# Four output groups in another order, and seven gate multiplications on GpSimd instead of VectorE

## The chip, the cores and the metric

The kernel runs on one core of a Trainium2 chip. The metric is the device time of one execution in microseconds (us), lower being better. The core's engines work side by side, each through its own queue in order: TensorE (PE in the profile, with PEld for its weight loads), VectorE (DVE), ScalarE (ACT), GpSimd (POOL) and SyncE (SP), which here only issues DMAs. A queue's own waiting and issuing is written with a q (SPq).

## What is computed

The input x has 2048 positions of 512 numbers in bfloat16. It is normalised, goes through two blocks side by side, and their sum is added to x:

```
xn = layernorm(x)
A: qkv = xn @ wqkv;  32 heads of 16; each position attends to 8 positions, 0, 2, ... 14 back
   o = softmax(q k / 4) v;           A = o @ wo
B: z = gelu(xn @ w_in)               (1376 wide, two halves of 688)
   z1 = first half;  z2 = layernorm(second half)
   g = w_sp @ z2 + b_sp              (w_sp is 2048 x 2048, mixing positions)
   B = (z1 * g) @ w_out              (688 to 512)
out = x + A + B
```

## The kernel before

Positions are worked in 16 tiles of 128. What matters here is the last third: the mixing of positions, the second half of the attention, and the output.

**Order.** Every step is a named operation, written down by `op_(name, needs, f)`. Five hand-written lists, `pe`, `act`, `dve`, `pool` and `sp`, hold the order of each engine's queue (lines 594 to 641). An engine works through its list in order; if one step waits, those behind it in the list wait too. The letters used below are the names in these lists.

**Mixing and gates.** `M{j}` (line 479) are the 32 matmuls of tile j of w_sp @ z2, into one of three PSUM tiles (`mm`). `G{j}` (ScalarE, line 495) adds the bias and copies the result to one of three gate buffers (`gs`), so `G{j}` needs `g{j-3}` done. `g{j}` (line 497) multiplies the gate with z1, 128 x 688 in bfloat16, in place in `z1u`; before the change all 16 are VectorE's. `U{j}` (line 484) is a DMA transpose, issued by SP, of the product into `uT`, with the 688 features on partitions: five full blocks of 128 and a rest of 48. `V{th}{g}` (line 490) are small DMAs that spread the rest rows over four partition groups (`rest`): those of the first half of the positions (th = 0) are issued by GpSimd, those of the second half by SP.

**Attention.** The positions are two halves, th = 0 and 1. VectorE multiplies the attention weights with the values and sums them in twelve steps `a{th}.0` to `a{th}.11` (lines 430, 434 and 443). The last, line 443, writes `op`, which lies in the place of `xnT`; the profile shows it by that name. All operands are in SBUF. Between these steps stand the `g{j}` in VectorE's list.

**Output.** The 16 output tiles are four groups of four; group n = 2 th + s. Each tile of a group has its own PSUM bank; groups 0 and 2 share four banks, groups 1 and 3 the other four. A tile is the sum of three parts:
- the full gated part (`gated_full`, line 533): five matmuls over 128 x 512 from `uT` and `w_out`;
- the gated rest (line 540): two small matmuls per tile with 32 and 16 rows;
- the attention part (line 544): 16 small matmuls per tile with 32 rows from `op` and `wo`. The small matmuls of a group's four tiles stand at four row positions of the array.

In the old order PE's list ends with gf0 gf1 ao0 ao1 gf2 ao2 ao3 gf3: full parts of groups 0 and 1; rest and attention parts of 0 and of 1; full part of 2; rest and attention of 2 and of 3; the full parts of group 3, whose last tile is done in three column pieces (`gfl0` to `gfl2`, line 567) in banks that have come free. `ao{n}` holds rest and attention parts together. ScalarE copies the finished groups 0 and 1 out (`E{i}`, line 578), and VectorE adds x to the copies (`F{i}`, line 579); for groups 2 and 3 VectorE adds x straight from PSUM (line 584). VectorE's additions stand behind all attention steps in its list. SP stores each tile (line 585).

Of the kernel before, what the change touches and what calls it, by code (L numbers as in the profile page):

```python
# [10 lines left out]
ALU = mybir.AluOpType  # L11
# [5 lines left out]
NT = S // P  # L17
# [9 lines left out]
FH = 688  # L27
F = 2 * FH
# [14 lines left out]
def kernel(  # L43
# [13 lines left out]
    V = nc.vector  # L57
    A = nc.scalar
    G = nc.gpsimd
# [23 lines left out]
    b16 = sb.tile([NT, P], BF16, name="b16")  # L83
# [21 lines left out]
    gs = [qk_r[0][:, (MF + 1) * HS + n * FH:(MF + 1) * HS + (n + 1) * FH] for n in range(3)]  # L105
# [8 lines left out]
    z1u = z1_r[:].rearrange("p (i f) -> p i f", i=NT)  # L114
# [38 lines left out]
    def op_(name, after, f):  # L153
        assert name not in do, name
        do[name], needs[name] = f, list(after)
# [48 lines left out]
    def psum(kind, writer, reader, after, f):  # L204
        pool = mm if kind == "mm" else aux
        n = len(ring[kind])
        t = pool[n % len(pool)]
        old = [ring[kind][n - len(pool)]] if n >= len(pool) else []
        ring[kind].append(reader)
        op_(writer, list(after) + old, lambda: f(t))  # L210
        return t
# [90 lines left out]
    for i in range(NT):  # L302
        g = i // 4 * 4
# [77 lines left out]
    for c, th in BUF:  # L381
        n = f"{c}{th}"
# [92 lines left out]
    def mix(t, j):  # L475
        w = wsp[(j // 2) % 3]
        for k in range(NT):
            for hh in range(2):
                PE.matmul(t[:, hh, 0:FHALF], w[:, k, (j % 2) * P:(j % 2 + 1) * P],  # L479
                          z2[:, k, hh * FHALF:(hh + 1) * FHALF], start=(k == 0), stop=(k == NT - 1))  # L480

    def turn_u(j):
        th, t0 = j // 8, (j % 8) * P
        SP.dma_start_transpose(uT[th][:, :, t0:t0 + P], z1u[:, j, :])
# [7 lines left out]
    def make_M(j):  # L492
        t = psum("mm", f"M{j}", f"G{j}", [f"zn{x}" for x in range(NT)] + [f"W{j // 2}", "Bc"], lambda t: mix(t, j))
        op_(f"G{j}", [f"M{j}"] + [f"m{c}{t}" for c in (0, 1) for t in (0, 1)] + ([f"g{j - 3}"] if j >= 3 else []),
            lambda: A.activation(gs[j % 3].rearrange("p (a b) -> p a b", a=2), t[:, :, 0:FHALF], ACT.Identity,  # L495
                                 bias=b_col[:, j:j + 1]))
        op_(f"g{j}", [f"G{j}", f"yg{j}"], lambda: V.tensor_tensor(z1u[:, j, 0:FH], gs[j % 3], z1u[:, j, 0:FH], ALU.mult))
        op_(f"U{j}", [f"g{j}"] + [f"m{c}{t}" for c in (j // 8 * 2, j // 8 * 2 + 1) for t in (0, 1)], lambda: turn_u(j))


# [26 lines left out]
    groups = [[8 * th + 2 * g + t for g in range(4)] for th in range(2) for t in range(2)]  # L527
    po = {i: banks[4 * (n % 2) + g] for n, tiles in enumerate(groups) for g, i in enumerate(tiles)}

    def gated_full(i, start, stop, c=slice(0, D)):  # L530
        th, t0 = i // 8, (i % 8) * P
        for m in range(MF):
            PE.matmul(po[i][:, c], uT[th][:, m, t0:t0 + P], wout[:, m, c], start=(start and m == 0), stop=(stop and m == MF - 1))  # L533

    def attention_out(n, start, stop):
        th, s = n // 2, n % 2
        for r in range(2):
            for g in range(4):
                p = slice(32 * g, 32 * g + RN[r])
                PE.matmul(po[groups[n][g]], rest[th][r][p, s * P:(s + 1) * P], wrest[r][p, :],  # L540
                          start=(start and r == 0), stop=False, tile_position=(32 * g, 0))
        for d in range(DH):
            for g in range(4):
                PE.matmul(po[groups[n][g]], op[32 * g:32 * g + 32, th, d, s * P:(s + 1) * P], wo_r[32 * g:32 * g + 32, d, :],  # L544
                          start=False, stop=(d == DH - 1 and (stop or groups[n][g] == groups[3][3])), tile_position=(32 * g, 0))

    U = [[f"U{j}" for j in range(8 * th, 8 * th + 8)] for th in range(2)]
    EVM = [f"G{j}" for j in range(NT)] + ["Bc", "Tc4"]
    for n in (0, 1):
        op_(f"gf{n}", LO + U[0] + EVM, lambda n=n: [gated_full(i, True, False) for i in groups[n]])  # L550
        op_(f"ao{n}", [f"gf{n}", "a0.11"] + [f"V0{g}" for g in range(4)], lambda n=n: attention_out(n, False, True))
    op_("gf2", U[1] + [f"E{i}" for i in groups[0]], lambda: [gated_full(i, True, False) for i in groups[2]])
    V1 = [f"V1{g}" for g in range(4)]
    op_("ao2", ["gf2", "a1.11"] + V1, lambda: attention_out(2, False, True))
    op_("ao3", U[1] + [f"E{i}" for i in groups[1]] + ["a1.11"] + V1, lambda: attention_out(3, True, False))

    parts = [slice(0, D // 2), slice(D // 2, 3 * D // 4), slice(3 * D // 4, D)]
    pieces = [(banks[n][:, 0:c.stop - c.start], c) for n, c in zip((0, 2, 5), parts)]
    early = stmp[:, 0:2].rearrange("p a s -> p (a s)")
    tail = [groups[3][g] for g in (0, 1, 2)]  # L560
# [11 lines left out]
    def o_of(i):  # L572
        return ot[i]

    for n in range(4):
        for i in groups[n]:
            if n < 2:
                op_(f"E{i}", [f"ao{n}"], lambda i=i: A.copy(o_of(i), po[i]))  # L578
                op_(f"F{i}", [f"E{i}", "R0"], lambda i=i: V.tensor_tensor(o_of(i), o_of(i), xr[0][:, i % 8, :], ALU.add))
            else:  # L580
                if i == groups[3][3]:
                    continue
                op_(f"F{i}", ["ao2" if n == 2 else f"gf3.{i}", "R1"],
                    lambda i=i: V.tensor_tensor(o_of(i), po[i], xr[1][:, i % 8, :], ALU.add))
            op_(f"S{i}", [f"F{i}"], lambda i=i: SP.dma_start(out2[i * P:(i + 1) * P, :], o_of(i)))

# [2 lines left out]
    for n, (t, c) in enumerate(pieces):  # L589
# [5 lines left out]
        k0 k1 q0 q1 k2 k3 q2 q3 k4 k5 q4 q5 k6 k7 q6 q7  # L595
        v0 v1 v2 v3 v4 v5 v6 v7 z15 y2 y3 y4 y5 y6 y7 y8 y9 y10 y11 y12 y13 y14 y15
        M0 M1 M2 M3 M4 M5 M6 M7 M8 M9 M10 M11 M12 M13 M14 M15
        gf0 gf1 ao0 ao1 gf2 ao2 ao3""".split() + [f"gf3.{i}" for i in tail] + ["gfl0", "gfl1", "gfl2"]
    for n in pe:
        a, x = n[0], n[1:]  # L600
        if n in do:
            continue
        if n == "T0a":
            make_T0()
        elif a == "T":
            make_T(int(x))
        elif n == "z0a":
            make_z0()
        elif a == "z":
            make_z(int(x))  # L610
        elif a == "y":
            make_y(int(x))
        elif a in "qkv":
            make_heads(a, int(x))
        elif a == "M":
            make_M(int(x))
        elif a == "B":
            make_B()
# [10 lines left out]
    for i in range(6, NT):  # L629
        dve += [f"ag{i + 1}"] * (i + 1 < NT) + [f"b{i + 2}"] * (i + 2 < NT) + [f"n{i}"]  # L630
    dve += """zt0 zt1 zt2 zt3 zt4 zt5 zn0 zn1 zn2 zn3 zt6 zt7 zn4 zn5 zn6 zn7
        m00 f00 p00 m01 zs8 m10 m11 zb8 p01 m20 p10 m21 p11 zs12 m30 p20 zb12 m31 p21 p30 X0 p31 HW u0 X1 C0 g0 a0.0 u1 a0.1 C1 g1 g2
        a0.2 g3 a0.3 g4 a0.4 g5 a0.5 a0.6 g6 a0.7 g7 a0.8 a0.9 g8 a0.10 a0.11 g9 g10 a1.0 a1.1 g11 a1.2 g12 a1.3
        a1.4 g13 a1.5 g14 a1.6 a1.7 g15 a1.8 a1.9 a1.10 a1.11""".split()
    OUT = [i for n in range(3) for i in groups[n]] + tail
    dve += [f"F{i}" for i in OUT[:12]] + ["Fe"] + [f"F{i}" for i in OUT[12:]] + ["Fl0", "Fl1", "Fl2"]
    pool = ["b16"] + [f"gr{i}" for i in range(NT)] + "zr0 zr4 kh2 f01 zr8 f10 kh3 f11 f20 f21 zr12 f30 f31 LO5 V00 V01 V02 V03".split()
    sp = """x0 x1 x2 x3 x4 x5 x6 x8 wy x12 wk wq wv t8 t9 t10 t11 t12 t13 t14 t15 W0 kh0a kh0b W1 kh1 vh
        W2 W3 LO0 LO1 W4 U0 W5 LO2 LO3 U1 U2 W6 LO4 U3 U4 W7 U5 U6 U7 U8 U9 U10 R0 U11 U12 U13 V10 V11 R1 U14 V12 U15 V13""".split()
    sp += [f"S{i}" for i in OUT] + ["Sl0", "Sl2"]  # L640
# [53 lines left out]
```

## Time and profile before

| what | value |
|---|---|
| time, median of 3 runs | 200.33 us (200.26 to 200.45) |
| time of the profiled execution | 200.27 us |
| its span, first to last event of the engines | 198.5 us |
| instructions | 4606 |
| granted clock of TensorE | full in all slices |

The profile is of one execution. Its page gives for each engine the busy time and share of the span, then the chain of work that ended last with its shares by engine. A row of the timeline has the start in us from the span's start, the duration in us of the merged run of instructions, engine, line of the program, operation, output and inputs by name, shapes and count; square brackets hold idle time before it and what ended it. A row of the groups has the count, then busy time in us and mean ns of one, then idle time before it. A row of a line's instructions has the shortest, median and longest duration in ns and the first and last start. Some matmul records are missing from the trace, so a count can be a few short. A row of the DMA issues ends with KB each and the median us from issue to landing.

### The profile page before, as it was taken

How to read it: one execution, taken by the hardware profiler on the slowest of the kernel's cores; microseconds unless marked ns; L12 is line 12 of the kernel's file. 1: busy time of each engine (PE TensorE's matmuls, PEld its weight loads, DVE VectorE, ACT ScalarE, POOL GpSimd, SP SyncE). 2: the span in 40 equal slices, each digit the busy share in tenths (PEclk: the TensorE clock that was granted, in tenths of full speed). 3: DMA queues.
4: the chain of work that ended last, by engine and by line, in shares of the span. 5: the costliest groups of instructions: out<-in, count | busy, mean ns of one | idle time of the engine just before them, and what ended most of it. 6: DMA issues, size and time to landing. Idle time of an engine off the chain costs nothing.

```text
span 198.5 us, 4606 instructions
## 1 busy us (share of the span) xinstructions
PE 194.2 (98%) x1957; PEld 122.0 (61%) x1960; DVE 178.4 (90%) x205; ACT 89.4 (45%) x130; POOL 49.3 (25%) x83
## 2 busy tenths in 40 slices
PE   8999999999999999999999999999999999999993
PEld 2566666666666666666666666666666654444442
DVE  4899896999979999988999999999999999997244
ACT  2587797875559885991462311111222110044000
POOL 5567222005992249363000000010111000000000
PEclk9999999999999999999999999999999999999999
DMA  5999566860979999998299999999999969204233
GB/s 156 355 363 212 102 135 137 96 131 6 182 141 173 204 168 179 169 181 162 48 229 229 165 220 236 193 181 225 262 185 109 242 116 259 45 3 147 68 106 106
DMA packets 69076, 32.87 MB, mean 166 GB/s; under 512 B 57312, under 2 KB 67072, under 8 KB 68928
## 3 DMA queue, kind: packets, MB, share of 16 engines
q1 hardware_dynamic: 65680, 24.15, 58.2%
q0 software_dynamic: 2688, 7.70, 21.2%
q10 hardware_dynamic: 688, 0.74, 1.3%
q8 instruction: 15, 0.25, 0.5%
q14 instruction: 5, 0.04, 0.1%
HBM read 10.13 MB, written 2.10 MB: 62 GB/s over the span
## 4 chain that ended last, share of the span: by engine, by line
PE 94%; DMA 2%; DVE 1%; issue 1%; POOL 0%; SPq 0%; DVEq 0%
PE mm L479 38%; PE mm L325 21%; PE mm L234 18%; PE mm L544 7%; PE mm L533 6%; PE aux L533 2%; DMA z<-in_A_x_dram 2%; PE mm L540 1%; PE aux L216 1%; SPq L166 0%; DVE stats L173 0%; DVE z L590 0%; POOL rstd L180 0%; DVE z L183 0%; POOL rstd L179 0%
## 5 line engine op out<-in xcount | busy, mean ns | idle before, releaser
L479 PE MATMUL mm<-z,wsp 128*128 128x344 bf16 x512 | 74.8, 309 | 0.0
L479 PEld LDWEIGHTS <-wsp 128*128 128x128 bf16 x512 | 50.1, 98 | 24.6
L325 PE MATMUL mm<-xnT,wts 128*32 128x512 bf16 x768 | 41.7, 379 | 0.0
L234 PE MATMUL mm<-wts,xnT 128*128 128x344 bf16 x256 | 38.8, 309 | 0.0
L325 PEld LDWEIGHTS <-wts 128*32 128x32 bf16 x768 | 28.5, 138 | 13.0 <-issue 0.3
L430 DVE TENSOR_TENSOR prod<-vp,a_sb 128x4096 bf16<-128x4096 bf16 x16 | 36.2, 2283 | 0.0
L495 ACT ACTIVATE qk<-mm,b_col 128x688 bf16<-128x688 f32 x16 | 13.2, 830 | 42.8 <-PE mm L479 41.3
L234 PEld LDWEIGHTS <-xnT 128*128 128x128 bf16 x256 | 24.7, 98 | 11.8 <-issue 0.4
L363 DVE TENSOR_TENSOR prod<-qk 128x4096 bf16<-128x4096 bf16 x12 | 26.9, 2287 | 0.3 <-ACT qk L338 0.2
L434 DVE TENSOR_TENSOR prod<-prod,prod 128x8192 bf16<-128x8192 bf16 x6 | 26.5, 4420 | 0.1
L338 ACT CAST qk<-mm 128x1024 bf16<-128x1024 f32 x16 | 16.2, 1012 | 8.2 <-PE mm L325 8.2
L490 POOL DMA_DIRECT2D qk<-qk x8 | 3.9, 496 | 54.2 <-DMA qk<-z 49.6
L544 PE MATMUL mm<-wts,xnT 32*128 32x512 bf16 x192 | 14.5, 374 | 0.0
L314 ACT ACTIVATE z<-mm 128x688 bf16<-128x688 f32 x16 | 11.6, 744 | 3.4 <-PE mm L234 3.0
L533 PEld LDWEIGHTS <-qk 128*128 128x128 bf16 x75 | 7.2, 98 | 9.1 <-issue 0.8
L251 ACT ACTIVATE z<-mm 128x688 bf16<-128x688 f32 x16 | 11.9, 745 | 1.8 <-PE mm L234 1.8
L533 PE MATMUL mm<-wts,qk 128*128 128x512 bf16 x52 | 12.2, 379 | 0.3 <-issue 0.2
L173 DVE BATCH_NORM_STATS2 stats<-z 128x6 f32<-128x512 bf16 x16 | 10.7, 671 | 1.7 <-DMA z<-in_A_x_dram 1.7
L371 POOL DMA_DIRECT2D prod<-prod x10 | 9.4, 1132 | 8.4 <-DVE prod L363 8.4
L544 PEld LDWEIGHTS <-xnT 32*128 32x128 bf16 x256 | 6.5, 93 | 7.3
L578 ACT CAST z<-mm 128x512 bf16<-128x512 f32 x6 | 3.3, 600 | 13.7 <-PE mm L544 13.7
L338 ACT CAST vp<-mm 128x1024 bf16<-128x1024 f32 x8 | 8.1, 1011 | 2.7 <-PE mm L325 2.7
(92 smaller groups left out, 186.9 us busy)
## 6 DMA issues: line engine op xcount, KB each, us to landing
prod<-prod POOLq DMA_DIRECT2D x10, 512.0 KB, 8.5
wts<-in_A_wo_dram SPq DMA_DIRECT2D x4, 512.0 KB, 6.7
wsp<-in_A_x_dram SPq DMA_DIRECT2D x2, 1024.0 KB, 6.1
out_dram<-z SPq DMA_DIRECT2D x15, 128.0 KB, 1.8
wts<-in_A_wqkv_dram SPq DMA_DIRECT2D x3, 512.0 KB, 8.8
z<-in_A_x_dram SPq DMA_DIRECT2D x2, 512.0 KB, 6.4
wsp<-z POOLq DMA_DIRECT2D x2, 512.0 KB, 7.1
wsp<-wts POOLq DMA_DIRECT2D x2, 512.0 KB, 9.4
```

The lines of the kernel that those rows point to most:

```text
L234: PE.matmul(t[:, hh, 0:FHALF], xnT[:, kc, i * P:(i + 1) * P], w_z[part][:, kc, hh * FHALF:(hh + 1) * FHALF], start=(kc == 0), stop=(kc == ...
L251: A.activation(z2[:, i, :].rearrange("p (a b) -> p a b", a=2), t[:, :, 0:FHALF], ACT.Gelu_apprx_tanh, **total)
L314: op_(f"yg{i}", [f"y{i}"], lambda: A.activation(z1u[:, i, 0:FH].rearrange("p (a b) -> p a b", a=2), t[:, :, 0:FHALF], ACT.Gelu_apprx_tanh))
L325: PE.matmul(t[32 * g:32 * g + 32, dd, :], w, r, start=(kc == 0), stop=(kc == C - 1), tile_position=(0, 32 * g))
L338: op_(f"{a}c{p}", [f"{a}{p}"], lambda: A.copy(home(a, p), t[:].rearrange("p d (t s) -> p d t s", t=2)))
L363: V.tensor_tensor(pr, q, k, ALU.mult)
L430: return lambda: V.tensor_tensor(dst, vp[:, :, th, off:off + GS], a_sb[:, th, W - 1 - w].unsqueeze(1).broadcast_to([P, DH, GS]), ALU.mult)
L434: return lambda: V.tensor_tensor(dst, dst, x, ALU.add)
L479: PE.matmul(t[:, hh, 0:FHALF], w[:, k, (j % 2) * P:(j % 2 + 1) * P], z2[:, k, hh * FHALF:(hh + 1) * FHALF], start=(k == 0), stop=(k == NT ...
L495: lambda: A.activation(gs[j % 3].rearrange("p (a b) -> p a b", a=2), t[:, :, 0:FHALF], ACT.Identity, bias=b_col[:, j:j + 1]))
L533: PE.matmul(po[i][:, c], uT[th][:, m, t0:t0 + P], wout[:, m, c], start=(start and m == 0), stop=(stop and m == MF - 1))
L544: PE.matmul(po[groups[n][g]], op[32 * g:32 * g + 32, th, d, s * P:(s + 1) * P], wo_r[32 * g:32 * g + 32, d, :], start=False, stop=(d == DH ...
```

## The change

Three things are changed:

1. `attention_out` is split in two: `gated_rest` (`re{n}`) and `attention_out` (`ao{n}`). For groups 0 and 1 the order of the matmuls stays.
2. For groups 2 and 3 the order becomes: rest and attention part of 2, rest and attention part of 3, then the full parts of group 2 tile by tile (`gf2.{i}`), then those of group 3. The small parts of group 2 now begin its sums, and its full parts end them. VectorE's additions for group 2 wait for the full part of their own tile.
3. `g9` to `g15` are issued on GpSimd, each between the spreads `V00` to `V03` in its list, and leave VectorE's list.

```diff
-        op_(f"g{j}", [f"G{j}", f"yg{j}"], lambda: V.tensor_tensor(z1u[:, j, 0:FH], gs[j % 3], z1u[:, j, 0:FH], ALU.mult))
+        op_(f"g{j}", [f"G{j}", f"yg{j}"], lambda: (V if j < 9 else G).tensor_tensor(z1u[:, j, 0:FH], gs[j % 3], z1u[:, j, 0:FH], ALU.mult))
...
-    def attention_out(n, start, stop):
+    def gated_rest(n, start):
         th, s = n // 2, n % 2
         for r in range(2):
             for g in range(4):
                 p = slice(32 * g, 32 * g + RN[r])
                 PE.matmul(po[groups[n][g]], rest[th][r][p, s * P:(s + 1) * P], wrest[r][p, :],
                           start=(start and r == 0), stop=False, tile_position=(32 * g, 0))
+
+    def attention_out(n, stop):
+        th, s = n // 2, n % 2
         for d in range(DH):
...
-        op_(f"ao{n}", [f"gf{n}", "a0.11"] + [f"V0{g}" for g in range(4)], lambda n=n: attention_out(n, False, True))
-    op_("gf2", U[1] + [f"E{i}" for i in groups[0]], lambda: [gated_full(i, True, False) for i in groups[2]])
-    V1 = [f"V1{g}" for g in range(4)]
-    op_("ao2", ["gf2", "a1.11"] + V1, lambda: attention_out(2, False, True))
-    op_("ao3", U[1] + [f"E{i}" for i in groups[1]] + ["a1.11"] + V1, lambda: attention_out(3, True, False))
+        op_(f"re{n}", [f"gf{n}"] + [f"V0{g}" for g in range(4)], lambda n=n: gated_rest(n, False))
+        op_(f"ao{n}", [f"re{n}", "a0.11"], lambda n=n: attention_out(n, True))
+    for n in (2, 3):
+        op_(f"re{n}", [f"V1{g}" for g in range(4)] + [f"E{i}" for i in groups[n - 2]], lambda n=n: gated_rest(n, True))
+        op_(f"ao{n}", [f"re{n}", "a1.11"], lambda n=n: attention_out(n, False))
+    for i in groups[2]:
+        op_(f"gf2.{i}", U[1] + ["ao2"], lambda i=i: gated_full(i, False, True))
...
-                op_(f"F{i}", ["ao2" if n == 2 else f"gf3.{i}", "R1"],
+                op_(f"F{i}", [f"gf{n}.{i}", "R1"],
...
-        gf0 gf1 ao0 ao1 gf2 ao2 ao3""".split() + [f"gf3.{i}" for i in tail] + ["gfl0", "gfl1", "gfl2"]
+        gf0 gf1 re0 ao0 re1 ao1 re2 ao2 re3 ao3""".split() + [f"gf2.{i}" for i in groups[2]] + [f"gf3.{i}" for i in tail] + ["gfl0", "gfl1", "gfl2"]
...
-        a0.2 g3 a0.3 g4 a0.4 g5 a0.5 a0.6 g6 a0.7 g7 a0.8 a0.9 g8 a0.10 a0.11 g9 g10 a1.0 a1.1 g11 a1.2 g12 a1.3
-        a1.4 g13 a1.5 g14 a1.6 a1.7 g15 a1.8 a1.9 a1.10 a1.11""".split()
+        a0.2 g3 a0.3 g4 a0.4 g5 a0.5 a0.6 g6 a0.7 g7 a0.8 a0.9 g8 a0.10 a0.11 a1.0 a1.1 a1.2 a1.3
+        a1.4 a1.5 a1.6 a1.7 a1.8 a1.9 a1.10 a1.11""".split()
...
-    pool = ["b16"] + [f"gr{i}" for i in range(NT)] + "zr0 zr4 kh2 f01 zr8 f10 kh3 f11 f20 f21 zr12 f30 f31 LO5 V00 V01 V02 V03".split()
+    pool = ["b16"] + [f"gr{i}" for i in range(NT)] + "zr0 zr4 kh2 f01 zr8 f10 kh3 f11 f20 f21 zr12 f30 f31 LO5 g9 V00 g10 V01 g11 V02 g12 V03 g13 g14 g15".split()
```

## The prediction, as it was made

> **What bounds the kernel now.** I read the page first: busy shares, then the chain that ended last.
>
> ```profile
> PE 194.2 (98%) x1957; PEld 122.0 (61%) x1960; DVE 178.4 (90%) x205; ACT 89.4 (45%) x130; POOL 49.3 (25%) x83
> ...
> PE 94%; DMA 2%; DVE 1%; issue 1%; POOL 0%; SPq 0%; DVEq 0%
> ```
>
> TensorE (PE) is busy 98% of the span and is 94% of the chain. VectorE (DVE) stands at 90%, and GpSimd (POOL) has three quarters of its time free. Next I read the timeline of PE from the end of the spatial mixing (162.0 us) on.
>
> ```profile
> 162.04 5.56 PE L533 MATMUL mm<-wts,qk 128*128 128x512 bf16 x24
> ...
> 170.77 0.39 PE L540 MATMUL mm<-wts,qk 32*128 32x512 bf16 x4
> ...
> 171.22 3.62 PE L544 MATMUL mm<-wts,xnT 32*128 32x512 bf16 x64
> ...
> 178.66 4.49 PE L533 MATMUL mm<-wts,qk 128*128 128x512 bf16 x19
> 183.09 0.39 PE L540 MATMUL mm<-wts,qk 32*128 32x512 bf16 x4
> 183.31 0.39 PE L540 MATMUL mm<-qk 16*128 16x512 bf16 x4
> 183.53 3.62 PE L544 MATMUL mm<-wts,xnT 32*128 32x512 bf16 x64
> 186.99 0.37 PE L540 MATMUL mm<-wts,qk 32*128 32x512 bf16 x1
> ...
> 191.20 1.03 PE L533 MATMUL mm<-wts,qk 128*128 128x512 bf16 x4 [0.16 <-issue]
> ...
> 195.05 0.44 PE L567 MATMUL aux<-wts,qk 128*128 128x128 bf16 x5
> ```
>
> This is the output in the old order: full gated tiles (L533) for groups 0 and 1, then their small parts (L540 and L544), then from 178.66 the full tiles of group 2, from 183.09 its small parts, from 186.99 those of group 3, and the tail. Nothing stands between the rows but 0.16 us of issue: PE never waits for DVE. The last matmul ends at 195.05 + 0.44 = 195.49. The profiled execution took 200.27 us, so 4.78 us lie behind that, and it stands 0.06 us below the median of 200.33; I make the sum on 200.27.
>
> The timeline of DVE shows how near DVE is:
>
> ```profile
> 131.62 4.48 DVE L430 TENSOR_TENSOR prod<-vp,a_sb 128x4096 bf16<-128x4096 bf16 x2
> 136.02 0.51 DVE L497 TENSOR_TENSOR z<-qk,z 128x688 bf16<-128x688 bf16 x1
> ...
> 143.18 0.94 DVE L497 TENSOR_TENSOR z<-qk,z 128x688 bf16<-128x688 bf16 x2
> 144.03 4.49 DVE L430 TENSOR_TENSOR prod<-vp,a_sb 128x4096 bf16<-128x4096 bf16 x2
> ...
> 172.81 4.42 DVE L434 TENSOR_TENSOR prod<-prod,prod 128x8192 bf16<-128x8192 bf16 x1
> 177.34 2.29 DVE L443 TENSOR_TENSOR xnT<-prod 128x4096 bf16<-128x4096 bf16 x1
> 179.55 2.77 DVE L579 TENSOR_TENSOR z<-z,wsp 128x512 bf16<-128x512 bf16 x8
> ```
>
> The second half's attention ends with L443 at 177.34 + 2.29 = 179.63. Its readers, the L544 matmuls of group 2, begin at 183.53. So 3.9 us of slack exist, made by the 4.43 us of full tiles between 178.66 and 183.09.
>
> **PE's new order.** No matmul is added or removed: four groups of 8 + 64 small ones, four times four tiles of five (less the split last tile). The full tiles of group 2 move from 178.66 to behind the small parts of group 3. What it saves is one change between small parts and full tiles. The 40 full matmuls of groups 0 and 1 took 170.77 - 162.04 = 8.73 us, 0.218 each; 20 at that pace are 4.37 us, against 4.43 taken from 178.66 to 183.09. With the 0.16 of issue the gain is bounded by 0 and 0.22 us, and I take 0.1. The price is the cover: the L540 part of group 2 now starts at 178.66 and takes 0.44 us (183.09 to 183.53), so PE wants the result of L443 at **179.10** instead of 183.53. Left as it is, DVE would be 0.5 us late.
>
> The other waits of this place are met. The banks of group 2 need the copies of group 0, and the rest rows need their spreads:
>
> ```profile
> 174.88 2.05 ACT L578 CAST z<-mm 128x512 bf16<-128x512 f32 x4 [11.80 <-PE mm L544]
> ...
> 171.36 1.15 SPq L490 DMA_DIRECT2D qk<-qk  x2
> ...
> qk<-qk SPq DMA_DIRECT2D x4, 16.0 KB, 1.9
> ```
>
> The copies end at 176.93. The last spread is issued by 172.51 and lands some 1.9 us later, near 174.4; both are ahead of 178.66. The copies of group 1 are wanted only at the small parts of group 3, 3.9 us later. The residual additions of group 2 (L584) now follow each full tile, about 1.1 us apart, instead of coming four at once. One takes 0.68 us, so DVE keeps pace, and the last pieces behind them are the same as before. I cost this at nothing; if DVE were late there, it would cost one addition, 0.6 us.
>
> **The seven multiplications taken from DVE.** In the rows above two of them fill 143.18 to 144.03, 0.43 us each. Seven are 3.0 us, all ahead of the last L443, as DVE runs without a gap. Alone, that moves its end from 179.63 to **176.6**, 2.5 us ahead of 179.10.
>
> **The seven multiplications given to GpSimd.** No row shows a large two-input operation on GpSimd. The nearest are one-input rows with 128 elements per partition, and tiny ones that met a busy DVE:
>
> ```profile
> L136 POOL TENSOR_SCALAR_AFFINE_SELECT ident<-ident 128x128 bf16<-128x128 bf16 x1 | 0.3, 283 | 0.1
> L678 POOL MEMSET const-float32-1.0<- 128x1 f32 x1 | 0.1, 103 | 0.0
> L271 POOL TENSOR_SCALAR zvar<-zmv 128x4 f32<-128x4 f32 x2 | 0.4, 195 | 9.1 <-DVE zmv L267 9.1
> L272 POOL TENSOR_TENSOR zrstd<-zvar,mhalf 128x4 f32<-128x4 f32 x2 | 2.0, 1017 | 0.2
> L288 POOL TENSOR_SCALAR zvar<-zvar 128x4 f32<-128x4 f32 x2 | 4.0, 1987 | 1.1 <-DVE zvar L284 1.0
> L289 POOL TENSOR_TENSOR zrstd<-zvar,mhalf 128x4 f32<-128x4 f32 x2 | 5.9, 2955 | 0.2
> ```
>
> Duration: 283 ns scaled by 688 / 128 is 1.52 us. With the 103 ns of a one-element row taken off as fixed cost, 180 ns x 5.4 = 0.97 us, and that is for one input. A second input makes it longer, so I take **1.5 us** (bounds 1.0 and 1.8, the upper an estimate, a fifth above the scaled row).
>
> Does it cost DVE time? The same two forms took 195 and 1017 ns in a stretch where DVE ran one-input statistics, and 1987 and 2955 ns beside DVE's two-input products. The timelines of both engines show what they waited for:
>
> ```profile
> 73.92 4.49 DVE L363 TENSOR_TENSOR prod<-qk 128x4096 bf16<-128x4096 bf16 x2
> 78.33 1.22 DVE L378 TENSOR_TENSOR prod<-prod 128x2048 bf16<-128x2048 bf16 x1
> ```
>
> ```profile
> 74.07 2.19 POOL L288 TENSOR_SCALAR zvar<-zvar 128x4 f32<-128x4 f32 x1 [1.03 <-DVE zvar L284]
> 76.35 2.95 POOL L289 TENSOR_TENSOR zrstd<-zvar,mhalf 128x4 f32<-128x4 f32 x1
> ```
>
> The first of the two products ends near 76.2 (half of 4.49 us behind 73.92), and L288 ends at 76.26. The second ends at 78.41, and L289 ends 0.89 us later, its usual length. So a GpSimd instruction that reads does not get at its data until the two-input DVE instruction in progress has ended. L378 behind it was not lengthened, but that GpSimd instruction read only four elements. With 688 elements in two streams the reading is nearly the whole instruction. If the two engines exclude each other, DVE stands still for about its length: a loss d per multiplication of 0 to 1.8 us. I take 1.5, because exclusion is what the rows show in the one direction that they can show. The Trainium skill, "SBUF — State Buffer", section "Who interferes with whom", states that a VectorE instruction with two SBUF inputs contends with a GpSimd instruction that reads SBUF, and that the loser blocks for the whole instruction. The trace agrees for GpSimd as the loser (2955 against 1017 ns); no row has DVE as the loser. From 4497 ns for 2048 elements in "GPSIMD Engine Reference", section 3.1, an estimate of the length is 1.5 us, and the sum would be the same.
>
> All seven fall before the last L443: the gate G15 of the last tile is done early, and GpSimd's queue has room.
>
> ```profile
> L479 PE MATMUL mm<-z,wsp x512: 309/309/309, 87.4 to 161.9; 128*128 128x344 bf16 x171
> ...
> 162.25 0.83 ACT L495 ACTIVATE qk<-mm,b_col 128x688 bf16<-128x688 f32 x1 [3.83 <-PE mm L479]
> ...
> 167.87 0.51 DVE L497 TENSOR_TENSOR z<-qk,z 128x688 bf16<-128x688 bf16 x1
> ...
> 132.30 0.98 POOL L490 DMA_DIRECT2D qk<-qk  x2 [37.29 <-DMA qk<-z]
> 141.31 0.98 POOL L490 DMA_DIRECT2D qk<-qk  x2 [8.03 <-DMA qk<-z]
> ```
>
> A tile of the mixing brings one gate per about 4.7 us (16 tiles from 87.4 to 162). GpSimd needs for it the wait for DVE's instruction (up to 4.4 us, half of it on average), 1.5 us, and 0.98 us for the two spreads interleaved with it: about 4.7 at most times, and three gate buffers absorb the rest. The spreads queued behind a multiplication are wanted at 170.77 only. On SP's queue the order stays, and the transposes of tiles 9 to 15 wait for GpSimd in place of DVE. The last gate is ready at 163.08, multiplied by 163.08 + 4.42 + 1.5 = 169.0 at worst, where DVE ended it at 168.4; the last spread then lands near 175.0, ahead of 178.66.
>
> **The sum.** L443 ends at 176.6 + 7 x 1.5 = 187.1; PE wants it at 179.1 and has nothing else in its order, so it stands still 8.0 us. 200.27 + 8.0 - 0.1 = 208.2. Then PE starts from rest, and the only start from rest in the trace is the first:
>
> ```profile
> 0.77 4.42 PE L463 MATMUL aux<-const-bfloat16-1.0 128*128 128x512 bf16 x10 [0.77 <-PEq L678]
> ```
>
> Ten matmuls of 512 columns took 4.42 us there, 2.2 us more than ten at the late pace of 0.22 us, though the page prints the granted clock as full. After 8 us of rest the loss lies between 0 and 2.2; I take 2.2, the row being the only one. **Forecast: 210.4 us**, with its own range of 206 to 212.6 (d from 1.2 to 1.8, with or without the slow start). The Trainium skill, "TensorE: Matmul & The Clock Gate", Part 1, halves the clock after an idle window of about 3.4 us; no row here shows it within a run.
>
> **The rivals.**
> - *DVE is not held back* (the other side): GpSimd's reads slip in between DVE's, as the four elements before L378 did. L443 ends at 176.6, PE never waits, and only the switch counts: 200.2 us. It decides below d = (179.1 - 176.6) / 7 = 0.35 us. For it: L378's plain 1.22 us. Against it: the whole waits of L288 and L289.
> - *DVE is held back in part*: d of 0.35 to 1.2 us, because GpSimd is quicker than the scaled row or holds the reads in bursts. PE waits 7d - 2.5 us: 0 to 5.9, hence 200.2 to 206, and up to 208 with a slow start.
> - *GpSimd starves*: it loses each time until DVE is done. Then gate 12 lacks its buffer, which g9 holds, mixing 15 lacks its PSUM, and PE stops near 157. g9 runs at 176.6 to 178.1, G12 ends at 179, mixing 15 at 183.7, where before it ended at 162.0: 21.7 us later, about 222. For it: DVE has no gap. Against it: L288 and L289 got in at the first end of an instruction.
> - *The order gains more than a switch*, 0.4 us or more: the rows leave only 0.22.
>
> **How the numbers follow.** Chances: forecast 0.45, held in part 0.22, not held 0.22, starved 0.07, better order 0.04. About 0.2% (0.4 us) is what a measurement of this kernel can tell from no change. Faster: 0.04. Same: not held and the lowest edge of in part, 0.22 + 0.02 = 0.24. Slower: 0.72. The range must reach the case of no hold, 200.0 to 200.3, and the top of the forecast: 199.9 to 212.6 leaves out starvation and the better order.
>
> **What would show it.** In the changed profile the L430 and L434 rows after 134 us should have a few at 3.7 to 6 us in place of 2.28 and 4.42, each beside a L497 row on POOL; the last L443 should end near 187; PE should show one idle time of about 8 us ahead of L544 of group 2, released by DVE, and matmuls behind it at half pace for some 4 us. If the DVE rows keep their lengths, d is 0 and the first rival holds. If POOL's rows last many us and ACT's L495 waits for them, it is starvation. The forecast is wrong if GpSimd's multiplication takes under 0.5 us or does not exclude DVE.

## The result, and the profile after it

The changed kernel took 208.68 us (median of 4 runs, 208.51 to 209.4) against 200.39 us; the ratio is 1.0421, with a 95% interval of 1.0398 to 1.0444. It is slower by 4.2%. The profiled execution took 208.51 us, 8.24 us more than that of before. The page, in the same order as before:

```profile
PE 196.5 (95%) x1958; PEld 122.8 (59%) x1960; DVE 184.3 (89%) x198; ACT 89.4 (43%) x130; POOL 74.4 (36%) x90
...
DVE 55%; PE 27%; DMA 9%; POOL 4%; issue 3%; ACT 0%; DVEq 0%
```

DVE has lost seven instructions (205 to 198) and is busy 5.9 us longer, and the chain has passed from PE to DVE. PE's timeline at the output (L547 is the line of the attention part now):

```profile
161.78 5.56 PE L533 MATMUL mm<-wts,qk 128*128 128x512 bf16 x24
...
178.52 0.39 PE L540 MATMUL mm<-qk 16*128 16x512 bf16 x4
185.08 5.99 PE L547 MATMUL mm<-wts,xnT 32*128 32x512 bf16 x64 [6.18 <-DVE xnT L443]
...
195.12 5.34 PE L533 MATMUL mm<-wts,qk 128*128 128x512 bf16 x24 [0.16 <-issue]
...
203.28 0.44 PE L572 MATMUL aux<-wts,qk 128*128 128x128 bf16 x5
```

Two numbers make the difference: PE stands 6.18 us until the last L443 of DVE, and the 64 matmuls behind it take 5.99 us instead of 3.62, 2.37 more. Three small terms complete the sum. Matmuls that follow one another overlap in these rows (the row at 178.52 lasts 0.39 us, and where PE does not wait the next row starts 0.22 us behind it), so a wait costs 0.17 us more than the idle time that is shown. The new order gives 0.22 us back: from the first L533 of the output to the end of the last matmul PE takes 33.23 us in each of the four kernels below that have the new order and do not wait, and 33.45 us before the change. And PE came to the output 0.26 us earlier in this execution (161.78 against 162.04). 6.18 + 0.17 + 2.37 - 0.22 - 0.26 = 8.24. Behind the last matmul lie 4.79 us, as before (4.78).

Why L443 is late is in the timelines of DVE and of GpSimd:

```profile
135.85 4.42 DVE L434 TENSOR_TENSOR prod<-prod,prod 128x8192 bf16<-128x8192 bf16 x1
140.37 3.39 DVE L443 TENSOR_TENSOR xnT<-prod 128x4096 bf16<-128x4096 bf16 x1
143.80 13.93 DVE L430 TENSOR_TENSOR prod<-vp,a_sb 128x4096 bf16<-128x4096 bf16 x4
157.76 4.42 DVE L434 TENSOR_TENSOR prod<-prod,prod 128x8192 bf16<-128x8192 bf16 x1
162.22 6.96 DVE L430 TENSOR_TENSOR prod<-vp,a_sb 128x4096 bf16<-128x4096 bf16 x2
...
182.73 2.29 DVE L443 TENSOR_TENSOR xnT<-prod 128x4096 bf16<-128x4096 bf16 x1
```

```profile
134.90 6.71 POOL L497 TENSOR_TENSOR z<-qk,z 128x688 bf16<-128x688 bf16 x1 [40.49 <-ACT qk L495]
141.56 1.05 POOL L490 DMA_DIRECT2D qk<-qk  x2
142.63 2.48 POOL L497 TENSOR_TENSOR z<-qk,z 128x688 bf16<-128x688 bf16 x1
145.06 1.04 POOL L490 DMA_DIRECT2D qk<-qk  x2
146.12 2.48 POOL L497 TENSOR_TENSOR z<-qk,z 128x688 bf16<-128x688 bf16 x1
```

Seven DVE instructions are stretched: one L443 (3.39 us, elsewhere 2.29), four L430 (13.93 us, undisturbed about 8.9) and two more (6.96, undisturbed 4.49). Each stretched one starts while a multiplication on GpSimd is at work. GpSimd's 142.63 begins in the middle of the L443 that ends at 143.76, waits for that end, and is done at 145.11; the L430 started at 143.80 pays for it. They take turns.

Last, the clock. The rows of stretches give from and to, length, busy time of PE, PEld, DVE, ACT and POOL with counts, the granted clock as a share of full speed, DMA share and GB/s:

```profile
178.90:182.00 3.10, 0.00 (x1) 0.00 (x0) 3.10 (x1) 1.68 (x4) 0.00 (x0) 1.00 0.00 0
182.00:185.00 3.00, 0.00 (x0) 0.00 (x0) 2.90 (x3) 0.00 (x0) 0.00 (x0) 0.68 0.00 0
185.08:187.00 1.92, 1.92 (x20) 0.74 (x24) 1.92 (x7) 0.00 (x0) 0.00 (x0) 0.50 0.33 110
187.00:189.00 2.00, 2.00 (x24) 0.72 (x20) 0.71 (x3) 0.00 (x0) 0.00 (x0) 0.50 0.81 268
189.00:190.00 1.00, 1.00 (x16) 0.36 (x12) 0.00 (x0) 0.00 (x0) 0.00 (x0) 0.55 0.80 267
190.00:191.00 1.00, 1.00 (x24) 0.48 (x20) 0.00 (x0) 0.00 (x0) 0.00 (x0) 1.00 0.10 33
```

In the second half of the rest the granted clock falls, and it stays at 0.50 until nearly 190, some 5 us into the work. The 0.55 of the row from 189 to 190 puts the change at 189.9; half of the 4.8 us worked until then is 2.4 us, the 2.37 us that the 64 matmuls took longer.

### The profile page after: what moved, and what is told of

Its sections match the earlier page's. It is cut to its first block, busy times and chain, and to the rows that moved or that the text cites. A ratio compares the mean times of both kernels' runs of the same rounds, so it can differ in the third digit from the quotient of the medians.

```text
span 206.7 us, 4611 instructions
## 1 busy us (share of the span) xinstructions
PE 196.5 (95%) x1958; PEld 122.8 (59%) x1960; DVE 184.3 (89%) x198; ACT 89.4 (43%) x130; POOL 74.4 (36%) x90
## 4 chain that ended last, share of the span: by engine, by line
DVE 55%; PE 27%; DMA 9%; POOL 4%; issue 3%; ACT 0%; DVEq 0%
DVE prod L430 21%; DVE prod L434 13%; PE mm L234 9%; PE mm L325 8%; PE mm L547 5%; DMA wsp<-z 4%; DMA prod<-prod 4%; DVE prod L363 4%; DVE xnT L443 3%; PE mm L533 3%; DVE a_sb L379 2%; DVE z L497 2%; DVE prod L378 2%; POOL prod L371 1%; DVE stmp L406 1%
## 5 line engine op out<-in xcount | busy, mean ns | idle before, releaser
L430 DVE TENSOR_TENSOR prod<-vp,a_sb 128x4096 bf16<-128x4096 bf16 x16 | 43.5, 2753 | 0.1
L497 POOL TENSOR_TENSOR z<-qk,z 128x688 bf16<-128x688 bf16 x7 | 24.8, 3554 | 43.8 <-ACT qk L495 43.7
L434 DVE TENSOR_TENSOR prod<-prod,prod 128x8192 bf16<-128x8192 bf16 x6 | 26.5, 4422 | 0.1
L547 PE MATMUL mm<-wts,xnT 32*128 32x512 bf16 x192 | 16.8, 434 | 6.2 <-DVE xnT L443 6.2
L547 PEld LDWEIGHTS <-xnT 32*128 32x128 bf16 x256 | 6.9, 102 | 15.6 <-DVE xnT L443 6.7
L589 DVE TENSOR_TENSOR z<-mm,wsp 128x512 bf16<-128x512 f32 x5 | 3.3, 686 | 10.4 <-PE mm L533 10.4
L533 PEld LDWEIGHTS <-qk 128*128 128x128 bf16 x75 | 7.3, 98 | 8.9 <-issue 0.4
L533 PE MATMUL mm<-wts,qk 128*128 128x512 bf16 x53 | 12.1, 379 | 0.2 <-issue 0.2
L180 POOL TENSOR_TENSOR rstd<-rstd,mhalf 128x1 f32<-128x1 f32 x16 | 9.0, 561 | 1.3
```

What stands on the lines that cost most here:

```text
L430: return lambda: V.tensor_tensor(dst, vp[:, :, th, off:off + GS], a_sb[:, th, W - 1 - w].unsqueeze(1).broadcast_to([P, DH, GS]), ALU.mult)
L434: return lambda: V.tensor_tensor(dst, dst, x, ALU.add)
L497: op_(f"g{j}", [f"G{j}", f"yg{j}"], lambda: (V if j < 9 else G).tensor_tensor(z1u[:, j, 0:FH], gs[j % 3], z1u[:, j, 0:FH], ALU.mult))
```

## Experiments

The theory under test: (a) while GpSimd reads its operands, a two-input VectorE instruction stands still, so that each gate moved costs DVE more than it saves; (b) the new order has used up the slack, so PE pays for what DVE loses; (c) a long enough rest of PE lowers its clock. The rivals: the order itself costs the time, or GpSimd's own lateness does.

DVE reaches the stage up to 2.6 us apart in the profiles of the twelve kernels, one execution each, whose lists are nearly the same up to there (the L434 before the first half's L443 starts between 135.04 and 137.68), while PE's start of the output agrees within 0.5 us (161.78 to 162.25). So I also compare the stretch from the start of that L434 to the end of the last L443, which is free of this: 179.63 - 136.45 = 43.18 us before the change, 185.02 - 135.85 = 49.17 us in the changed kernel.

### Each half of the change alone

The new order alone puts the gates back on VectorE:

```diff
-(V if j < 9 else G).tensor_tensor(z1u[:, j, 0:FH], gs[j % 3], z1u[:, j, 0:FH], ALU.mult)
+V.tensor_tensor(z1u[:, j, 0:FH], gs[j % 3], z1u[:, j, 0:FH], ALU.mult)
...
-LO5 g9 V00 g10 V01 g11 V02 g12 V03 g13 g14 g15
+LO5 V00 V01 V02 V03
```

> The new output order with all 16 gates on VectorE. My theory (VectorE is held while GpSimd reads, and the new order has taken the cover away): the last attention step ends near 179.6 as before, TensorE wants it at 179.1, so it stands 0.5 us, and the change between small parts and full tiles gives 0.1 back: 200.7 us, between 200.3 and 200.9. Rival (the order itself costs the time, through banks, copies or spreads): most of the 8.2 us stays, about 208 us.

Measured: 200.74 us (median of 11), ratio 1.0028 (1.0011 to 1.0045). PE stood 0.61 us:

```profile
178.70 0.39 PE L540 MATMUL mm<-qk 16*128 16x512 bf16 x4
179.70 3.63 PE L547 MATMUL mm<-wts,xnT 32*128 32x512 bf16 x64 [0.61 <-DVE xnT L443]
```

The order alone costs 0.3%, no more. Its runs scatter from 199.91 to 201.49. I take this for DVE's variation, which reaches the end time where there is no slack; one of these executions has a profile, so it is not shown.

The gates alone keep the old order:

```diff
+(V if j < 9 else G).tensor_tensor(z1u[:, j, 0:FH], gs[j % 3], z1u[:, j, 0:FH], ALU.mult)
...
+LO5 g9 V00 g10 V01 g11 V02 g12 V03 g13 g14 g15
```

> The old output order with gates 9 to 15 on GpSimd. My theory: the last attention step ends at 185.0 as in the changed kernel, TensorE wants it at 183.3 to 183.5 behind the full tiles of group 2, so it stands 1.5 to 1.7 us, too short for the slow clock: about 202.0 us. Rival (GpSimd alone carries the loss, the order has no part): about 208 us.

Measured: 204.32 us in the median, 202.64 to 205.4 over 4 runs, ratio 1.0194 (1.0149 to 1.024). The profiled one took 202.64:

```profile
183.27 0.39 PE L540 MATMUL mm<-qk 16*128 16x512 bf16 x4
185.87 3.63 PE L544 MATMUL mm<-wts,xnT 32*128 32x512 bf16 x64 [2.21 <-DVE xnT L443]
```

Here theory and profile agree to 0.6 us, but the median missed by 2.3. Two of the runs (205.24 and 205.4) had a mean granted clock of 0.992, the others 1.0: with DVE a little later the rest may be long enough to lower the clock. There is no profile of those two executions, so this is not shown, and it has a rival: two of 22 executions of the old kernel also had a mean clock of 0.991, and took 202.02 and 202.13 us. The gates are the larger half of the change; the cover of the old order took up much of their loss.

### How the loss goes with the number of gates

Gates 13 to 15 on GpSimd, 9 to 12 on VectorE, new order (`j < 13`, lists accordingly):

> The new order with only gates 13 to 15 on GpSimd. My theory, in which each gate moved costs VectorE 1.28 us and saves it 0.43: the last attention step ends at 179.6 + 3 x 0.85 = 182.2, TensorE stands 3.1 us: 203.3 us with the clock kept, 205.6 if the slow clock comes after this rest too. Rival (the loss comes from a few late gates or a fixed start-up of GpSimd, not from each): under 201.5 or over 206 us.

Measured: 205.54 us (204.18 to 206.49), ratio 1.0257 (1.0218 to 1.0296).

```profile
154.25 5.59 DVE L434 TENSOR_TENSOR prod<-prod,prod 128x8192 bf16<-128x8192 bf16 x1
159.88 6.96 DVE L430 TENSOR_TENSOR prod<-vp,a_sb 128x4096 bf16<-128x4096 bf16 x2
```

```profile
182.74 5.32 PE L547 MATMUL mm<-wts,xnT 32*128 32x512 bf16 x64 [3.76 <-DVE xnT L443]
```

Three gates stretch three instructions, and the rest of 3.76 us was followed by slow matmuls. Here the clock fell only after PE had begun again (the row is in the part on the clock).

Gates 9 to 15 left out altogether (those tiles keep the ungated z1):

```diff
+V.tensor_tensor(z1u[:, j, 0:FH], gs[j % 3], z1u[:, j, 0:FH], ALU.mult) if j < 9 else None
```

> The new order with gates 9 to 15 left out altogether: those seven tiles keep the ungated z1, nothing else changes. My theory: VectorE is 3.0 us shorter and nobody holds it, the last attention step ends at 176.6, TensorE does not wait: 200.2 us, between 200.0 and 200.3. Rival (the new order needs more than the attention result in time): over 201 us.

Measured: 199.98 us (median of 12), ratio 0.9976 (0.9954 to 0.9998). PE did not wait:

```profile
135.04 4.42 DVE L434 TENSOR_TENSOR prod<-prod,prod 128x8192 bf16<-128x8192 bf16 x1
...
173.32 2.29 DVE L443 TENSOR_TENSOR xnT<-prod 128x4096 bf16<-128x4096 bf16 x1
```

```profile
179.03 3.62 PE L547 MATMUL mm<-wts,xnT 32*128 32x512 bf16 x64
```

With DVE early enough the new order is worth some 0.2%, and nothing else in it is late.

The stretch of DVE from L434 to the last L443 is now known for four kernels: 40.57 us without these gates (135.04 to 175.61), 43.18 with seven on VectorE, 45.79 with four on VectorE and three on GpSimd (136.89 to 182.68), 49.17 with seven on GpSimd. A gate on VectorE costs it 2.61 / 7 = **0.37 us**, one on GpSimd costs VectorE 8.60 / 7 = **1.23 us**; four and three give 40.57 + 1.49 + 3.69 = 45.75, and 45.79 was measured. The loss is per gate, with no fixed part that these four show.

### What GpSimd does to VectorE

The gate on GpSimd as a fill, writing the tile and reading nothing:

```diff
+V.tensor_tensor(z1u[:, j, 0:FH], gs[j % 3], z1u[:, j, 0:FH], ALU.mult) if j < 9 else G.memset(z1u[:, j, 0:FH], 0.0)
```

> The changed kernel with gates 9 to 15 on GpSimd as a fill of the same 128 x 688 tile with zeros: it writes and reads nothing, the multiplication is left out. My theory (what is shared is the reading): VectorE's steps keep 2.28 and 4.42 us, the last attention step ends near 176 to 176.6, about 200.2 us. Rival (any GpSimd instruction on SBUF holds VectorE): the steps beside a fill are longer by its length, about 0.5 us each, the last step ends near 180 and the time is about 201.

Measured: 199.86 us in one execution. The fills need no gate and so ran earlier than the multiplications did, but four of the seven (one from 147.42, three from 151.90) ran beside these DVE rows:

```profile
143.22 8.90 DVE L430 TENSOR_TENSOR prod<-vp,a_sb 128x4096 bf16<-128x4096 bf16 x4
152.16 4.42 DVE L434 TENSOR_TENSOR prod<-prod,prod 128x8192 bf16<-128x8192 bf16 x1
```

```profile
147.42 0.69 POOL L497 MEMSET z<- 128x688 bf16 x1
150.93 0.99 POOL L490 DMA_DIRECT2D qk<-qk  x2 [2.82 <-DMA qk<-z]
151.90 1.91 POOL L497 MEMSET z<- 128x688 bf16 x3
```

No stretching: writing alone does not hold DVE. One input instead of two, the gate times 1:

```diff
+V.tensor_tensor(z1u[:, j, 0:FH], gs[j % 3], z1u[:, j, 0:FH], ALU.mult) if j < 9 else G.tensor_scalar(z1u[:, j, 0:FH], gs[j % 3], 1.0, None, ALU.mult)
```

> The changed kernel with gates 9 to 15 on GpSimd as the gate times the constant 1, so with one input tile read instead of two; the multiplication by z1 is left out. My theory (VectorE stands while GpSimd reads): the loss per gate goes with the reading time, for one stream 0.5 to 0.9 us instead of 1.28, the last attention step ends at 176.3 + 7 x 0.7 = 181.2, TensorE stands 2.1 us: about 202.3 us. Rival (a fixed cost of the hand-over between the engines): 1.2 us per gate as before, about 208.5 us.

Measured: 204.59 us in one execution. The stretch of DVE is 44.61 us (137.41 to 182.02), so (44.61 - 40.57) / 7 = 0.58 us per gate, about half of 1.23: the loss goes with what GpSimd reads. It does not go with the length of GpSimd's instruction, for the one-input multiplication is not shorter:

```profile
144.62 10.92 DVE L430 TENSOR_TENSOR prod<-vp,a_sb 128x4096 bf16<-128x4096 bf16 x4
```

```profile
144.69 1.94 POOL L497 TENSOR_SCALAR z<-qk 128x688 bf16<-128x688 bf16 x1
```

None of the seven took less than 1.94 us, and VectorE went on through most of that time. The time missed because DVE came 1.6 us later than in the changed kernel and because a rest of 3.05 us was already followed by slow matmuls:

```profile
182.08 5.08 PE L547 MATMUL mm<-wts,xnT 32*128 32x512 bf16 x64 [3.05 <-DVE xnT L443]
```

Next the length of a gate by itself. Steps 0 to 10 of the second half's attention are left out, and VectorE is idle:

```diff
-(USES if n == 11 else []), f)
+(USES if n == 11 else []), f if th == 0 or n == 11 else (lambda: None))
```

> The changed kernel with steps 0 to 10 of the second half's attention left out, so that VectorE is idle while GpSimd multiplies gates 10 to 15. My theory: each of these takes 1.25 to 1.45 us, the time by which a VectorE step was lengthened (1.24) and a start-up of 0.1. Rival (GpSimd shares the port and both are slowed): clearly under 1.2 us. The time itself is bound by TensorE: 200.2 us.

Measured: 200.25 us, and gates 12 to 15 take 1.48 to 1.50 us, slightly above the bracket; 10 and 11 still met an L443.

```profile
151.43 1.50 POOL L497 TENSOR_TENSOR z<-qk,z 128x688 bf16<-128x688 bf16 x1
...
158.75 1.48 POOL L497 TENSOR_TENSOR z<-qk,z 128x688 bf16<-128x688 bf16 x1 [3.17 <-ACT qk L495]
```

VectorE is held for 1.23 of these 1.5 us. The same steps replaced by one-input statistics on VectorE:

```diff
+f if th == 0 or n == 11 else (lambda n=n: [V.bn_stats(zst[:, 0, 0, :], prod[0][:, k * D:(k + 1) * D]) for k in range(6 if n in (4, 7, 10) else 3)])
```

> The changed kernel with steps 0 to 10 of the second half's attention replaced by one-input statistics (128 x 512, three or six per step) on VectorE; that half's attention result is left out. My theory (the second input of a VectorE instruction and GpSimd's inputs exclude each other): beside the gates the statistics keep the 0.67 us that they take alone, and gates 11 to 15 take 1.5 us as beside an idle VectorE; TensorE does not wait, 200.2 us. Rival (any VectorE instruction that reads SBUF is held): some statistics last 1.9 us, one per gate, and gates wait for the end of one.

Measured: 199.99 us. Shortest, median and longest of the 42 statistics, and a gate beside them:

```profile
L449 DVE BATCH_NORM_STATS2 zst<-prod x42: 680/694/695, 145.3 to 175.2; 128x6 f32<-128x512 bf16 x42
```

```profile
150.24 1.50 POOL L497 TENSOR_TENSOR z<-qk,z 128x688 bf16<-128x688 bf16 x1
```

Neither engine feels the other, and PE does not wait although all seven gates are on GpSimd, so GpSimd's own lateness is not what costs the time. What excludes each other is VectorE's two-input steps and GpSimd's inputs, not the two engines as such. That it is the second input and nothing else in which the statistics differ from those steps (operation, output) was not tested by itself.

### The clock

In the changed kernel, 18 matmuls on constants are put into PE's wait:

```diff
+    op_("sp", ["re2"] + [f"E{i}" for i in groups[1]], lambda: [spin(po[groups[3][0]], D, 1) for _ in range(18)])
...
-re2 ao2 re3 ao3
+re2 sp ao2 re3 ao3
```

> The changed kernel with 18 matmuls on constants (128 x 512, results overwritten) put into TensorE's wait, behind the copies of group 1, from about 180.6 to 184.5. My theory (the rest of 6.2 us lowers the clock, and that alone lengthens the 64 small matmuls from 3.62 to 5.99 us): the wait stays, the granted clock stays full, the 64 matmuls take 3.6 us again, 208.5 - 2.3 = 206.2 us. Rival (the matmuls were slow for another reason, transfers of the output beside them for instance): 208.5 us.

Measured: 207.12 us (206.71 to 207.41), ratio 1.0334 (1.0312 to 1.0356).

```profile
180.81 4.10 PE L463 MATMUL mm<-const-bfloat16-1.0 128*128 128x512 bf16 x18 [1.72 <-ACT z L584]
186.32 3.63 PE L547 MATMUL mm<-wts,xnT 32*128 32x512 bf16 x64 [1.41 <-DVE xnT L443]
```

The 64 matmuls take 3.63 us again, at a granted clock of 1.00 and with the output's transfers beside them as before:

```profile
186.30:189.90 3.60, 3.58 (x68) 1.75 (x72) 2.64 (x8) 0.00 (x0) 0.00 (x0) 1.00 0.55 181
```

The median fell by 1.6 us and not 2.3. In the profiled execution the time fell by 1.1 us (208.51 to 207.37), because DVE came 1.4 us later (L434 at 137.22) and the last L443 ended 1.2 us later (186.26 against 185.02). The next kernel happens to be the changed one with DVE as late (L434 at 137.32): 210.14 us against the 207.37 us of this one's profiled execution, 2.8 us apart.

The low clock also gives the price of the other rests. These are the stretches in which PE worked at 0.50: with one input on GpSimd (after a rest of 3.05 us), with three gates there (3.76 us), and in that next kernel (7.32 us):

```profile
182.08:185.06 2.98, 2.98 (x32) 1.07 (x36) 2.63 (x8) 0.00 (x0) 0.00 (x0) 0.50 0.50 167
...
183.98:187.40 3.42, 3.42 (x40) 1.34 (x32) 1.38 (x5) 0.00 (x0) 0.00 (x0) 0.50 0.81 266
...
186.41:191.88 5.47, 5.47 (x52) 2.00 (x56) 2.63 (x8) 0.00 (x0) 0.00 (x0) 0.50 0.58 192
```

Half of each is 1.49, 1.71 and 2.74 us; the 64 matmuls took 1.46, 1.70 and 2.69 us longer than 3.62.

That next kernel puts one small multiplication on GpSimd ahead of gate 9, to see why gate 9 took 6.7 us or more:

```diff
+    op_("wm", ["g2"], lambda: G.tensor_tensor(z2_junk[:, 0:8], z2_junk[:, 8:16], z2_junk[:, 16:24], ALU.mult))
...
+LO5 wm g9 V00 g10 V01 g11 V02 g12 V03 g13 g14 g15
```

> The changed kernel with one small bfloat16 multiplication (128 x 8, on a scratch tile) on GpSimd behind gate 2, 20 us or more before gate 9. In the kernels so far gate 9 took 6.7 to 8.6 us and let two ends of VectorE instructions go by. My theory: a first-use cost of some us in GpSimd delays its first read, so now gate 9 takes at most 4 us and gets in at the first or second end; seven steps are held as before and the time stays, 207.5 to 209.5 us. Rival (gate 9 meets another obstacle at that place, its queue or VectorE's): still 6.5 to 8.6 us.

Measured: 210.14 us in one execution, and gate 9 still took 7.99 us, so a first use of the operation, taken away by one this small, is not the reason. Its row and those of VectorE:

```profile
135.08 7.99 POOL L497 TENSOR_TENSOR z<-qk,z 128x688 bf16<-128x688 bf16 x1 [38.58 <-ACT qk L495]
```

```profile
136.89 0.51 DVE L497 TENSOR_TENSOR z<-qk,z 128x688 bf16<-128x688 bf16 x1
137.32 4.41 DVE L434 TENSOR_TENSOR prod<-prod,prod 128x8192 bf16<-128x8192 bf16 x1
141.83 3.39 DVE L443 TENSOR_TENSOR xnT<-prod 128x4096 bf16<-128x4096 bf16 x1
```

Gate 9 lets two ends of VectorE instructions pass (136.97 and 137.40) and gets in at the third, before the L443; the later gates get in at the first. What sets this is open. It costs no time here, since one instruction is held either way.

## Why the prediction was right

Point by point:

- **No matmul added, a switch saved**: right. 0.22 us in the profiles of the kernels in which PE does not wait, 0.1 taken; the kernel without the gates is 0.24% below the old one (interval 0.02 to 0.46%). That the bound of 0.22 held is luck: the 0.16 us of issue in it stand beside a row that counts four of a tile's five matmuls (191.20, x4), and in the kernel with the fills, whose row counts all 25, no such idle time is shown. It is a record missing from the trace and not time of PE.
- **The cover is gone, PE wants L443 at 179.1**: right; with the order alone PE waited from 179.09 to 179.70.
- **Copies, spreads, additions of group 2, GpSimd's queue met in time**: right. In the runs without held steps PE waits for nothing.
- **3.0 us taken from DVE**: too much, 2.6 us. The 0.43 counted the start of a multiplication to the start of the next step. Where a multiplication stood between two steps, each began some 0.08 us before the one ahead had ended (143.18 against 143.26); where none does, the next step begins some 0.03 us behind the end (141.88 against 141.85 without the gates). That the steps then depend on one another directly is my reading of it.
- **GpSimd's length of 1.5 us**, scaled from a one-input row with 128 elements: right, 1.48 to 1.50, and by luck in part. The row is of another operation, and the step behind it, that a second input makes it longer, did not hold here: the one-input multiplication took no less than 1.94 us.
- **Loss d per gate of 1.5 us**: the mechanism right, the size too large, 1.23, at the lower end of the 1.2 to 1.8 that I allowed. I set the loss equal to the whole instruction; VectorE was held for 1.23 us of one of 1.5 and, with one input, for 0.58 us of one of 1.94. With the two terms L443 came out 7.5 us late on balance, and it was 6.0 (49.17 - 43.18). PE's rest was 6.2 us instead of 8.0; this is the 1.9 us by which the forecast of 210.4 is above the 208.51 of the profiled execution, but for a few tenths.
- **The slow start of 2.2 us**, from the first ten matmuls of the kernel: right, 2.37, and the kernel kept busy shows the cause. That the size came so near is luck in part: the row says how slow ten matmuls are, not how long the clock stays low, and behind other rests the loss was 1.46 to 2.69 us, which passes the bound of 2.2. The page of the Trainium skill, "TensorE: Matmul & The Clock Gate", Part 1, gives an idle window of about 3.4 us. Here a rest of 3.05 us was already followed by slow matmuls (5.08 us for 64) and one of 2.21 us was not (3.63), so a rest a little under that figure can be enough.
- **The rivals**: no hold falls with the stretched steps (1.23 against the 0.35 us at which it decides). The partial hold does not fall in kind: 1.23 is only 0.03 above the 1.2 at which I drew the line, and VectorE was held for a part of the instruction, not for all of it. Starvation falls: the gates got in. The better order falls: 0.22 us is less than 0.4. The Trainium skill's rule in "SBUF — State Buffer", "Who interferes with whom", is borne out in both directions, and for the fill and the one-input statistics too, which that section exempts. That the hold lasts a whole instruction is not borne out: it was 1.23 of 1.5 us with two inputs and 0.58 of 1.94 with one.

The step drawn from L288 and L289, that GpSimd waits for a two-input VectorE instruction, held for the two-input gates; some one-input ones did not wait (last section). That L378 behind them was not stretched said nothing on VectorE's side: at 1.23 us for 688 elements, an estimate for four is below 0.01 us.

No kernel here beats the old one and computes the whole: the new order's 0.2% needs the attention result earlier, by 0.6 us in the profile of the order alone and by more in executions in which VectorE comes later, by other means than reading on GpSimd. That was not tried.

## What to carry to other kernels

Before moving work from VectorE to GpSimd, look at the operands of what stays: it was free beside one-input statistics or when GpSimd only wrote, but beside two-input VectorE steps each 128 x 688 gate cost VectorE 1.23 us to save 0.37. Look at what the new order does with slack before taking it: 3.9 us of unused slack can take up VectorE's variation of one or two microseconds. And price a long wait of TensorE with the slow matmuls behind it, here 1.5 to 2.7 us more behind rests of 3.05 us and above and nothing behind 2.21 us.

## What was not expected of the hardware

- VectorE's start in this stage varies by up to 2.6 us between profiles of these kernels whose TensorE times agree within 0.5 us. Why is open.
- A GpSimd read waits sometimes for one and sometimes for three VectorE instructions to end (gate 9, 6.7 to 8.1 us in every kernel with the multiplication there), and some do not wait at all: with one input, the gates at 144.69, 147.65 and 155.60 began 0.03 to 0.12 us behind the start of a VectorE step and took 1.94 us. The cause is open.
- 64 matmuls of 3.62 us took 5.08, 5.32, 5.99 and 6.31 us behind rests of 3.05, 3.76, 6.18 and 7.32 us. The extra time is half of what PE worked at a clock of 0.50, and the moment at which the clock falls is not fixed by the rest: it came 2.6 us into the rest of 3.05 us, some 4 us into that of 6.18 us, and with three gates on GpSimd 1.2 us after PE had begun again.
